# First FFN stage of a fused attention and FFN kernel: 20 block products per 2x3x4 blocks in place of seven per 2x2x2

## The chip, the cores and the metric

One core of a Trainium2 chip runs the whole program. The metric is the time of one execution on the device in microseconds (us).

## The reference

Sigmoid attention over 8 batches of 12 heads, 448 positions and 64 channels, and behind it an FFN without bias on the 3584 tokens (768 to 2048 to 768) with a leaky ReLU, all in float32:

```python
scores = scale * np.matmul(q, k.transpose(0, 1, 3, 2)) - np.log(S)
attn = 1.0 / (1.0 + np.exp(-scores))
attn_out = np.matmul(attn, v)
x = attn_out.transpose(0, 2, 1, 3).reshape(B * S, H * D)
h = x @ w_in
g = np.maximum(0.01 * h, h)
return g @ w_out
```

## The kernel before

The program has three stages in a row. All three keep x, h and the result transposed: channels lie on the 128 partitions, the 448 tokens of a batch in the columns.

*Attention.* 24 rounds of five slots take two pairs of heads each. A round holds scores of two pairs (tiles `sc`, split operands `qks`), the sigmoids on ScalarE (ACT, tiles `s`), and the products with v (`pv`). In the slot after, ACT copies one bank of `pv` to x (`half`) and VectorE (DVE) adds the other bank (`keep`); both banks are then used for later scores. The four PSUM buffers of this stage rotate, so the scores of the next round wait for the two additions.

*Operands in two parts.* Matmuls of the FFN get each float32 operand as a high part (a cast on ACT, method `high`) and a low part (the rest, a subtraction on DVE, `low`), and sum three products: high by high, high by low, low by high. So a product of blocks costs three matmuls for each 128x128 weight block and 448 columns.

*Weights.* `prep` is a generator. It decodes both weight matrices in pieces of 384 elements (load `wr`, five DVE instructions into `wd`), forms sums of blocks, and stores all the forms that the fast schemes need in DRAM (`td` for w_in, `t2d` for w_out). A planner, `prepare` in the attention rounds and `fill` in the first FFN stage, runs as many of its steps in a slot as the time that it counts for DVE there allows. At the end of attention 44 of the 64 pieces are done.

*First FFN stage* (h = x w_in). Four quarters of two batches each; in a quarter four units of 512 columns of w_in. A unit is one 2x2x2 scheme with seven block products in place of eight (`ORDER`). A block has 3 x 128 channels of x, so a product is 2 halves x 3 block columns x 3 parts = 18 matmuls. Class `Quad` keeps the sums: products 0, 4, 3 and 2 share the PSUM tile `px`, product 1 has `py`, 5 and 6 `pz`. `Quad.done` reads partial sums out of PSUM to `c_h` tiles, by an ACT copy where an output begins and a DVE addition where it goes on. A leaky pass on ACT follows, and DVE forms the sums of h that the second FFN stage wants (`made`); all is stored in DRAM. `Operands` makes the sums of x. `Weights` loads a form (`wx`), casts and splits it: `advance` asks for loads eight half products ahead, casts three or four ahead and low parts two or three ahead.

*Second FFN stage.* 52 products of 36 matmuls each in the lanes `acc_A` and `acc_B`, with its own operand and weight queues.

Each engine takes its instructions in the order of the code: `later(n, ...)` puts work in the slot n after, `first=True` ahead of the other work there. All loads and nearly all stores go through the queue of SyncE (SP), in the order of the code as well.

Of the kernel before, what the change touches and what calls it, by code (L numbers as in the profile page):

```python
# [27 lines left out]
GG, OO, WW = 7, 8, (3, 3)  # L28
# [3 lines left out]
PACES = 4, 5, 4.2, 2.8, 2  # L32
TIMES = 1.92, 1.92, 2.33, 2.33, 1.66
PRODUCT, LESS, MOST = 1.8, 0.2, 4
SHORT, LONG, OVER = 0.34, 0.54, 0.1
HOLD, WAIT, REST = 2, 9, 3
FFN = 126
ALONE = 100
LATER = 4
IDLE = 8  # L40


LEFT, MORE, RIGHT = 8, 6, 13

# [59 lines left out]
def attn_ffn_kernel(ctx: ExitStack, tc: tile.TileContext, qk, v, w_in, w_out, out):  # L104
# [18 lines left out]
    NU = w_in.shape[0]  # L123
    HW = NC // 2 * P
    NB = NC // 2
# [5 lines left out]

    td = [tc.dram_tile([P, NOP, 2, HW], F32, name=f"t0_{u}") for u in range(NU // 2)]
    wide = NC // 2 * P
    t2d = tc.dram_tile([P, FORMS, KQ, wide], F32, name="t1")
    xd = [tc.dram_tile([P, NB, S], F32, name=f"xd_{n}") for n in range(4)]
# [7 lines left out]
    mm, dma = pinned(nc.tensor.matmul), pinned(nc.sync.dma_start)  # L143
# [3 lines left out]
    def counted(issue, a_us):  # L147

        def run(out, **kw):
            nonlocal queue  # L150
            queue += 0.14 + math.prod(out.shape[1:]) / a_us
            return issue(out=out, **kw)

        return run
# [30 lines left out]
    stage = left.enter_context(tc.tile_pool(name="stage", bufs=STAGE))  # L185
    ring = left.enter_context(tc.tile_pool(name="ring", bufs=RING))
    prepared = set()

    class Weights:
# [5 lines left out]
        def load(self):  # L195
            self.x = stage.tile([P, 2, HW], F32, tag="stage", name=f"wx{self.u}_{self.n}")
            assert {(0, 2 * self.u), (0, 2 * self.u + 1)} <= prepared
            dma(out=self.x, in_=td[self.u][:, PLACE[self.n]])

        def high(self):  # L200
            self.t = ring.tile([P, 2, 2, HW], F32R, tag="ring", name=f"w0_{self.u}_{self.n}")
            copy(out=self.t[:, :, 0], in_=self.x)

        def low(self):
            sub(self.t[:, :, 1], self.x, self.t[:, :, 0])

    class Wide:
# [6 lines left out]
        def load(self):  # L214
            self.t = self.pool.tile([P, 2, KQ, wide], F32R, tag="t2", name=f"w1_{self.k}")
            dma(out=self.t[:, 1].bitcast(F32), in_=t2d[:, self.form])

        def high(self):
            copy(out=self.t[:, 0], in_=self.t[:, 1].bitcast(F32))
            self.has_high = True  # L220

        def low(self):
            sub(self.t[:, 1], self.t[:, 1].bitcast(F32), self.t[:, 0])
            self.has_low = True

        def of(self, part, e, m):
            return self.t[:, part, e, m * P:m * P + P]

    def parts_mm(acc, w, cols, hi, lo, first, last):

        for n, (part, x) in enumerate(((0, hi), (0, lo), (1, hi))):
            mm(acc, lhsT=w[:, part, cols], rhs=x, start=first and n == 0, stop=last and n == 2,
               skip_group_check=True)

    class Quad:

        def __init__(self, psum, pool, tag, name, bufs, last=copy, tags=("px", "pz")):  # L240


            self.psum, self.pool, self.tag, self.name, self.bufs = psum, pool, tag, name, bufs
            self.last, self.tags = last, tags
            self.x = self.bank(tags[0], "px")

        def bank(self, tag, what):
            return self.psum(tag, f"{what}_{self.name}")[:, :, :S]

        def take(self, what, acc, how=copy):  # L250
            t = self.pool.tile([P, 2, S], F32, tag=self.tag, name=f"{what}_{self.name}", bufs=self.bufs)
            how(out=t, in_=acc)
            return t

        def into(self, n, e):

            if e == 0 and n == 1:
                self.y = self.bank(self.tags[1], "py")
            elif e == 0 and n == 5:
                self.z = self.bank(self.tags[1], "pz")  # L260
            acc = self.y if n == 1 else self.z if n in (5, 6) else self.x
            return acc[:, e], n in (0, 1, 5)

        def done(self, n):

            if n == 0:
                self.c11 = self.take("c11", self.x)
            elif n == 1:
                add(self.c11, self.c11, self.y)
                return 0, 0, self.c11  # L270
            elif n == 4:
                self.c21 = self.take("c21", self.x)
            elif n == 5:
                self.c22 = self.take("c22", self.z)
            elif n == 3:
                add(self.c22, self.c22, self.x)
                return 1, 1, self.c22
            elif n == 6:
                add(self.c21, self.c21, self.z)
                return 1, 0, self.c21  # L280
            elif n == 2:
                return 0, 1, self.take("c12", self.x, self.last)
# [12 lines left out]


    def shift(stack, name, size, side="left"):

# [893 lines left out]
```

## Time and profile before

| | |
|---|---|
| timed runs | 1028.29, 1028.59 (median), 1028.60 us |
| span of the profiled execution, first to last instruction | 1026.2 us |
| TensorE (PE) busy | 1021.9 us |
| DVE busy | 857.5 us |
| ACT busy | 597.4 us |
| moved by DMA | 301.1 MB, mean 293 GB/s |

The span leaves out what lies ahead of the first instruction and behind the last; the median of the timed runs is 2.4 us above it. The time of the profiled execution itself is not recorded apart from its span. "Busy" is the share of time in which an engine had at least one instruction in work. Matmuls overlap in the records, so their pitch is read from the number that start in a stretch. PEld is the load of weights into TensorE, a row of its own in the profile.

### The profile page before, as it was taken

What the parts mean: (1) busy time and instruction counts of PE and PEld (TensorE: products, weight loads), DVE (VectorE), ACT (ScalarE), POOL (GpSimd) and SP (SyncE); (2) the same over time, 40 slices, a digit from 0 to 9 for tenths busy, and PEclk for the clock granted to TensorE, in tenths of its full rate; (3) what the DMA queues carried; (4) which work ended last, traced back from release to release, by engine and by line L of the source; (5) the groups of instructions that cost most, each with busy time, mean ns of one, the idle gap of its engine ahead of it and who ended that gap; (6) DMA issues with size and microseconds to landing.
All of it is one profiled execution on the core that took longest, in us unless ns stands there. A gap on an engine that the chain in (4) does not pass through costs nothing.

```text
span 1026.2 us, 16360 instructions
## 1 busy us (share of the span) xinstructions
PE 1021.9 (100%) x6316; PEld 867.4 (85%) x6316; DVE 857.5 (84%) x1015; ACT 597.4 (58%) x634; POOL 0.3 (0%) x5
## 2 busy tenths in 40 slices
PE   9999999999999999999999999999999999999998
PEld 5555555556999999999999999999999999999998
DVE  5879989889998899898975657699988888899883
ACT  7888888887545555555555555564352535444440
POOL 0000000000000000000000000000000000000000
PEclk9999999999999999999999999999999999999999
DMA  8887778889899998989986878998688797767833
GB/s 311 297 296 273 272 255 273 301 299 347 283 311 324 303 297 312 341 319 409 331 298 217 294 281 322 390 403 293 216 283 286 278 414 290 285 220 253 311 113 135
DMA packets 113853, 301.10 MB, mean 293 GB/s; under 512 B 9712, under 2 KB 51696, under 8 KB 113776
## 3 DMA queue, kind: packets, MB, share of 16 engines
q1 hardware_dynamic: 111760, 295.52, 80.8%
q10 hardware_dynamic: 2016, 4.54, 1.2%
q8 instruction: 50, 0.82, 0.3%
q14 instruction: 27, 0.22, 0.1%
HBM read 203.16 MB, written 96.86 MB: 292 GB/s over the span
## 4 chain that ended last, share of the span: by engine, by line
PE 99%; DMA 0%; SPq 0%; DVE 0%; issue 0%; DVEq 0%
PE px_h L141 22%; PE acc_A L141 18%; PE acc_B L141 18%; PE pv L141 13%; PE pz_h L141 11%; PE sc L141 11%; PE py_h L141 6%; DMA v<-in_v 0%; PE acc_one L141 0%; SPq L141 0%; DVE o L141 0%; DVEq L1188 0%
## 5 line engine op out<-in xcount | busy, mean ns | idle before, releaser
L141 PE MATMUL px_h<-hi,w 128*128 128x448 f32 x768 | 223.0, 361 | 0.0
L141 PEld LDWEIGHTS px_h<-hi,w 128*128 128x128 f32 x768 | 143.9, 187 | 11.4 <-ACT x L141 0.7
L141 PE MATMUL acc_A<-gh,w 128*128 128x448 f32 x528 | 151.4, 361 | 0.0
L141 DVE TENSOR_TENSOR w<-wx,w 128x768 fp32r<-128x768 f32 x112 | 106.9, 954 | 46.3 <-ACT w L141 46.2
L141 PE MATMUL px_h<-lo,w 128*128 128x448 f32 x384 | 139.4, 363 | 0.0
L141 ACT ACTIVATE s<-sc 128x896 f32<-128x896 f32 x144 | 119.4, 934 | 17.3 <-PE sc L141 17.3
L141 PE MATMUL acc_B<-gh,w 128*128 128x448 f32 x416 | 119.4, 361 | 0.0
L141 PE MATMUL pv<-s,v 64*64 64x448 f32 x1152 | 114.0, 540 | 0.2 <-DMA v<-in_v 0.2
L141 PE MATMUL pz_h<-hi,w 128*128 128x448 f32 x384 | 112.7, 361 | 0.0
L141 PEld LDWEIGHTS acc_A<-gh,w 128*128 128x128 f32 x528 | 98.9, 187 | 7.3
L141 PEld LDWEIGHTS sc<-qks 64*128 64x128 f32 x876 | 79.5, 185 | 22.7 <-issue 16.2
L141 ACT CAST w<-wx 128x768 fp32r<-128x768 f32 x112 | 91.9, 833 | 11.0 <-DMA wx<-t 11.0
L141 PE MATMUL sc<-qks 64*128 64x448 f32 (+1 forms) x876 | 94.2, 365 | 0.0
L141 PEld LDWEIGHTS pv<-s,v 64*64 64x64 f32 x1152 | 41.7, 133 | 61.0 <-issue 47.0
L141 DVE TENSOR_TENSOR w<-w 128x1536 fp32r<-128x1536 f32 x52 | 91.1, 1752 | 0.0
L141 ACT ACTIVATE c_h<-c_h 128x896 f32<-128x896 f32 x48 | 45.8, 954 | 74.7 <-DVE c_h L141 74.7
L141 PE MATMUL acc_B<-g,w 128*128 128x448 f32 x328 | 84.8, 362 | 0.0
L141 PEld LDWEIGHTS acc_B<-gh,w 128*128 128x128 f32 x416 | 77.9, 187 | 5.7
L141 ACT CAST w<-w 128x1536 fp32r<-128x1536 f32 x52 | 76.8, 1478 | 0.8 <-DMA w<-t 0.8
L141 PEld LDWEIGHTS pz_h<-hi,w 128*128 128x128 f32 x384 | 71.9, 187 | 5.4
L141 PEld LDWEIGHTS px_h<-lo,w 128*128 128x128 f32 x384 | 72.1, 188 | 3.7
L141 DVE SCALAR_TENSOR_TENSOR wd<-wr,wd 128x384 int32<-128x384 int32 x128 | 71.3, 557 | 3.0
(96 smaller groups left out, 1618.9 us busy)
## 6 DMA issues: line engine op xcount, KB each, us to landing
wx<-t SPq DMA_DIRECT2D x112, 384.0 KB, 5.4
w<-t SPq DMA_DIRECT2D x52, 768.0 KB, 4.4
g<-g SPq DMA_DIRECT2D x34, 896.0 KB, 7.7
g<-c_h SPq DMA_DIRECT2D x60, 448.0 KB, 4.6
g<-s SPq DMA_DIRECT2D x48, 448.0 KB, 5.9
qk<-in_qk SPq DMA_DIRECT2D x46, 456.0 KB, 5.0
g1s<-g SPq DMA_DIRECT2D x18, 896.0 KB, 6.1
wr<-in_w_in SPq DMA_DIRECT2D x32, 384.0 KB, 5.0
```

Of the source, the lines that this page charges most:

```text
L141: return lambda *args, **kw: tc.keep_in_program_order(issue(*args, **kw))
```

## The change

The first FFN stage takes four batches at a time, so it has two halves in place of four quarters. A unit (512 columns of w_in) is now 2 x 3 blocks of w_in by 3 x 4 blocks of x, 24 block products in the plain way, and `PRODUCTS_IN` does them as 20. A block has 2 x 128 channels, so a product is 2 x 2 x 3 = 12 matmuls. Each entry of the table names the lane (a PSUM tile), the form of w_in, the sum of x (`XSUMS`), and the outputs to which the running sum in the lane is added or from which it is taken after this product. Lanes go on after a read, so the value read is a partial sum. There are four PSUM buffers for the five lanes of a unit.

Around it: 16 forms of w_in in place of 7 (`STEPS_IN`), a form being 512 elements a partition where it was 768; 20 sums of x for a half, and x tiles of 896 elements; decoding of two pieces at a time in the attention rounds, instruction by instruction in turn, and in the FFN stage some of its masks on ACT; all memory in named places; another planner (`prepare` in both stages), whose price of a DVE instruction is 0.08 us and 1/960 us an element.

```diff
-ORDER = 0, 1, 4, 5, 3, 6, 2
-NOP = len(ORDER)
-
-PLACE = {0: 1, 1: 2, 4: 3, 5: 4, 3: 5, 6: 6, 2: 0}
-RING, STAGE = 4, 4
-ST = 7
...
+BLOCKS_IN = 4, 5, 0, 1, 2, 3
+FORMS_IN = 16
+STEPS_IN = (
+    ("sum", 3, "sub", ("s", 0, 1), ("d", 2, 0), ("d", 3, 1)), ("sum", 2, "sub", ("s", 3, 1), ("d", 1, 0), ("d", 2, 2)),
+    ("sum", 2, "sub", ("s", 6, 1), ("d", 0, 0), ("d", 3, 2)), ("sum", 1, "sub", ("s", 5, 1), ("d", 3, 1), ("s", 1, 1)),
...
+PRODUCTS_IN = (
+    ("A", 12, 14, "-3"), ("B", 0, 13, ""), ("A", 2, 31, "+1"), ("C", 0, 15, "-5"), ("A", 7, 16, "-0"), ("B", 1, 17, "+0 +4"),
+    ("A", 6, 0, "-4"), ("D", 11, 3, "-7"), ("B", 1, 18, "+7"), ("A", 13, 12, "+5"), ("E", 8, 8, ""), ("E", 10, 4, "-0"),
+    ("C", 15, 27, "-6"), ("B", 14, 21, "+3"), ("E", 8, 20, "-2"), ("C", 10, 29, "-2"), ("B", 9, 25, "+2"), ("E", 4, 23, "-3"),
+    ("C", 5, 28, "-1"), ("B", 3, 2, "+6"))
+N_IN = len(PRODUCTS_IN)
+XSUMS = {
+    12: ("add", 1, 0), 13: ("add", 7, 3), 14: ("sub", 13, 4), 15: ("sub", 14, 5), 16: ("add", 12, 9), 17: ("add", 16, 8),
+    18: ("sub", 11, 17), 19: ("add", 10, 2), 20: ("sub", 19, 8), 21: ("sub", 19, 11), 22: ("sub", 21, 4), 23: ("add", 22, 7),
+    24: ("sub", 22, 5), 25: ("add", 24, 6), 26: ("sub", 25, 21), 27: ("add", 26, 2), 28: ("add", 27, 9), 29: ("add", 27, 5),
+    30: ("add", 16, 14), 31: ("sub", 30, 0)}
+XQUEUE = (
+    "s13 s14 h0 l0 h1 l1 s12 s16 s30 s31 h2 l2 s15 h3 l3 h4 l4 s17 h5 l5 h6 l6 h7 l7 s18 h8 l8 h9 l9 h10 l10 h11 l11 "
...
+            both = 2 - k % 2 if now < FFN else 1
...
+            chains = [decode(raws[at + n][0], dec[:, (k + n) * PIECE:(k + n + 1) * PIECE], at + n in bare) for n in range(both)]
+            while chains:
+                for x in list(chains):
+                    step = next(x, None)
+                    if step is None:
+                        chains.remove(x)
+                    else:
...
-        while at_high < len(w1) and w1[at_high][0] <= t + 3 + (t >= 7):
+        while at_high < highs:
             w1[at_high][1].high()
             at_high += 1
-        while at_low < len(w1) and w1[at_low][0] <= t + 2 + (t >= 7):
+        while at_low < lows:
             w1[at_low][1].low()
             at_low += 1
-        while at_load < len(w1) and w1[at_load][0] <= t + 8 and at_load < at_low + STAGE:
+        while at_load < min(loads, at_low + RAWS):
             w1[at_load][1].load()
             at_load += 1
...
-            t = (self.p + 1) * NU * NOP - len(self.todo)
-            u, n, e = self.todo.pop(0)
-            advance(t)
-            p = self.p
-            if n == ORDER[0] and e == 0:
-                self.quad = Quad(psum, st, "st", f"h{p}_{u}", ST, leaky)
-                self.c = Results()
-            quad, c = self.quad, self.c
-            w = w1[t // 2][1].t[:, e]
-            acc, first = quad.into(n, e)
-            hi, lo = self.ops.hi[n], self.ops.lo[n]
-            for kk in range(NB):
-                parts_mm(acc, w, slice(kk * P, kk * P + P), hi[:, kk], lo[:, kk], first and kk == 0, kk == NB - 1)
-            if e == 0:
+            n = self.n
+            self.n += 1
+            t = N_IN * (UI * self.p + self.u) + n
+            x_ops(t)
+            advance(before(t + 7), before(t + 3), before(t + 2))
+            lane = PRODUCTS_IN[n][0]
+            first = lane not in self.accs
+            if first:
+                bank = lanes.pop(0)
+                self.accs[lane] = bank, psum(bank, f"acc_{t}")
+            bank, acc = self.accs[lane]
+            w, b = of_product[t], blocks[self.p]
+            hi, lo = b.forms[n].hi, b.forms[n].lo
+            for e in range(2):
+                for kk in range(NB):
+                    cols = slice(kk * P, kk * P + P)
+                    for m, (a, x) in enumerate(((w.hi, hi), (w.hi, lo), (w.lo, hi))):
+                        mm(acc[:, e, :S], lhsT=a[:, e, cols], rhs=x[:, kk], start=first and kk == 0 and m == 0,
+                           stop=kk == NB - 1 and m == 2, skip_group_check=True)
+            if self.u == UI - 1:
+                b.used(n)
+            ends = all(x[0] != lane for x in PRODUCTS_IN[n + 1:])
+            later(1, lambda: self.read(n, acc, bank, ends), first=True)
+
+        def read(self, n, acc, bank, ends):
+            for x in PRODUCTS_IN[n][3].split():
+                sign, o = x[0], divmod(int(x[1:]), 4)
+                if o not in self.outs:
+                    i, t = o
+                    name = self.names[t // 2][i, t % 2]
+                    users = 1 + sum(name in y[2:] for y in self.sums[t // 2])
+                    r = self.outs[o] = Result(f"h{self.p}_{self.u}_{i}{t}", users)
+                    if sign == "+":
+                        copy(out=r.t, in_=acc[:, :, :S])
+                    else:
+                        act(out=r.t, in_=acc[:, :, :S], func=AF.Copy, scale=-1.0)
+                else:
+                    r = self.outs[o]
+                    (add if sign == "+" else sub)(r.t, r.t, acc[:, :, :S])
+                if self.last[o] == n:
+                    self.done(o, r)
+            if ends:
+                lanes.append(bank)
...
-    wi = moe_w_in.reshape(2, NC // 2, P, 2, NU, P).transpose(4, 2, 0, 3, 1, 5).reshape(NU, P, 4, HW)
-    wi = np.ascontiguousarray(wi[:, :, [1, 3, 0, 2]]).reshape(NU, P, 4 * HW).view(np.int64)
+    wi = moe_w_in.reshape(3, 2, P, 2, NU // 2, 2, P).transpose(4, 5, 2, 3, 0, 1, 6).reshape(NU, P, len(BLOCKS_IN), 2 * P)
+    wi = np.ascontiguousarray(wi[:, :, list(BLOCKS_IN)]).reshape(NU, P, 4 * HW).view(np.int64)
```

Where instructions stand. DVE, attention stage, the decoding of the third unit of w_in (`wr` is a raw piece, `wd` the decoded one; in the rows of the changed kernel `wde`; `qks` the low part of q and k). Before:

```order
L141 TENSOR_SCALAR wd_2_840<-wr_2_1_654 128x384
L141 TENSOR_SCALAR wd_2_840<-wd_2_840 128x384 x2
L141 SCALAR_TENSOR_TENSOR wd_2_840<-wr_2_1_654,wd_2_840 128x384 x2
L141 TENSOR_SCALAR wd_2_840<-wr_2_2_676 128x384
L141 TENSOR_SCALAR wd_2_840<-wd_2_840 128x384 x2
L141 SCALAR_TENSOR_TENSOR wd_2_840<-wr_2_2_676,wd_2_840 128x384
L141 TENSOR_TENSOR qks_913<-qk_754,qks_913 128x848
L141 SCALAR_TENSOR_TENSOR wd_2_840<-wr_2_2_676,wd_2_840 128x384
```

And of the change:

```order
L188 TENSOR_SCALAR wde_321<-wr_2_0_465 128x384
L188 TENSOR_SCALAR wde_321<-wr_2_1_467 128x384
L188 TENSOR_SCALAR wde_321<-wde_321 128x384 x4
L188 SCALAR_TENSOR_TENSOR wde_321<-wr_2_0_465,wde_321 128x384
L188 SCALAR_TENSOR_TENSOR wde_321<-wr_2_1_467,wde_321 128x384
L188 SCALAR_TENSOR_TENSOR wde_321<-wr_2_0_465,wde_321 128x384
L188 SCALAR_TENSOR_TENSOR wde_321<-wr_2_1_467,wde_321 128x384
L188 TENSOR_TENSOR qks_845<-qk_677,qks_845 128x848
```

Each instruction on a piece had the one before it on the same piece as its neighbour; now the other piece stands between them.

TensorE, the first products of the first FFN stage (`hi`, `lo` and `f` are x operands, `w` weights). Before, the end of the first product and the start of the second:

```order
L141 MATMUL px_h_0_3280<-hi_0_1066,w_0_0_3215 128x448 x2
L141 MATMUL px_h_0_3280<-lo_0_1135,w_0_0_3215 128x448
L141 MATMUL px_h_0_3280<-hi_0_1066,w_0_0_3215 128x448
L141 MATMUL py_h_0_3317<-hi_0_1322,w_0_1_3242 128x448
L141 MATMUL py_h_0_3317<-lo_0_1390,w_0_1_3242 128x448
L141 MATMUL py_h_0_3317<-hi_0_1322,w_0_1_3242 128x448 x2
```

And of the change, the first ten products, one row each:

```order
L188 MATMUL acc_3409<-f_0_1929,w_0_12_3338 128x448 x12
L188 MATMUL acc_3437<-f_0_2060,w_0_0_3357 128x448 x12
L188 MATMUL acc_3409<-f_0_2454,w_0_2_3400 128x448 x12
L188 MATMUL acc_3482<-f_0_2585,w_0_0_3357 128x448 x12
L188 MATMUL acc_3409<-f_0_2714,w_0_7_3435 128x448 x12
L188 MATMUL acc_3437<-f_0_2847,w_0_1_3455 128x448 x12
L188 MATMUL acc_3409<-f_0_2971,w_0_6_3477 128x448 x12
L188 MATMUL acc_3563<-f_0_3104,w_0_11_3499 128x448 x12
L188 MATMUL acc_3437<-f_0_3396,w_0_1_3455 128x448 x12
L188 MATMUL acc_3409<-f_0_3398,w_0_13_3542 128x448 x12
```

A product has 12 matmuls where it had 18, and the tile `acc_3409` (lane A) comes back after one other product three times.

ACT, the same place. Before:

```order
L141 COPY c_h_0_3310<-px_h_0_3280 128x896
L141 CAST hi_0_3312<-x_825 128x1344
L141 CAST w_0_5_3330<-wx_5_3240 128x2x384
L141 ACTIVATE c_h_0_3310<-c_h_0_3310 128x896
L141 CAST hi_0_3359<-x_446 128x1344
L141 CAST w_0_3_3361<-wx_3_3257 128x2x384
L141 COPY c_h_0_3372<-px_h_0_3280 128x896
```

And of the change (`h` is an output, `acc` its lane):

```order
L188 ACTIVATE h_0_03_3427<-acc_3409 128x896
L188 CAST f_0_3430<-x_606 128x896
L188 CAST f_0_3433<-x_470 128x896
L188 CAST w_0_7_3435<-wx_7_3368 128x512
L188 CAST w_0_1_3455<-wx_1_3403 128x512
L188 COPY h_0_01_3472<-acc_3409 128x896
L188 CAST w_0_6_3477<-wx_6_3405 128x512
L188 ACTIVATE h_0_11_3495<-acc_3482 128x896
```

Between two reads of one PSUM tile by ACT stood four passes, and now stand four shorter ones within two products of 12 matmuls.

## Rows read from the trace of the kernel before

**Rows 1.** The page: span; then busy us (share of the span) and instructions.

```profile
span 1026.2 us, 16360 instructions
...
PE 1021.9 (100%) x6316; PEld 867.4 (85%) x6316; DVE 857.5 (84%) x1015; ACT 597.4 (58%) x634; POOL 0.3 (0%) x5
```

**Rows 2.** The chain that ended last, in time: start us, us, what.

```profile
1.65 4.96 DMA v<-in_v
...
19.86 4.67 PE pv L141 x48
...
29.85 4.67 PE pv L141 x48
...
266.87 7.20 PE px_h L141 x36
```

**Rows 3.** Windows of the three stages: busy us of each engine, granted clock, DMA share, GB/s.

```profile
0.00:244.50 244.50, 243.56 (x2424) 138.65 (x2428) 204.45 (x391) 205.38 (x268) 0.30 (x5) 1.00 0.84 290
244.50:648.00 403.50, 403.50 (x2023) 377.74 (x2016) 332.85 (x437) 221.07 (x251) 0.00 (x0) 1.00 0.89 313
648.00:1026.00 378.00, 374.87 (x1875) 351.02 (x1873) 320.21 (x188) 170.91 (x116) 0.00 (x0) 1.00 0.75 276
```

**Rows 4.** The waits: who for whom, us in total, times, longest us.

```profile
ACT c_h L141 <- DVE c_h L141: 74.7, 45, 2.6
...
DVE qks L141 <- ACT qks L141: 21.5, 22, 4.1
...
ACT w L141 <- DMA wx<-t: 11.0, 8, 2.7
...
PEld pv L141 <- ACT s L141: 8.8, 27, 0.5
...
PEld px_h L141 <- ACT x L141: 0.7, 1, 0.7
```

**Rows 5.** Windows of an attention round and of seven products; columns as in rows 3.

```profile
124.80:134.70 9.90, 9.90 (x108) 5.56 (x104) 9.69 (x19) 8.34 (x12) 0.00 (x0) 1.00 0.72 245
...
446.10:471.30 25.20, 25.20 (x127) 23.62 (x127) 23.56 (x35) 14.18 (x16) 0.00 (x0) 1.00 0.96 359
```

**Rows 6.** Groups of DVE by shape: count, busy us, mean ns, idle before.

```profile
L141 DVE TENSOR_TENSOR w<-wx,w 128x768 fp32r<-128x768 f32 x112 | 106.9, 954 | 46.3 <-ACT w L141 46.2
...
L141 DVE TENSOR_TENSOR lo<-x,hi 128x1344 fp32r<-128x1344 f32 x24 | 37.2, 1552 | 1.0 <-ACT hi L141 1.0
...
L141 DVE TENSOR_TENSOR x<-x,pv 128x448 f32<-128x448 f32 x48 | 27.6, 616 | 4.7 <-PE pv L141 4.3
...
L141 DVE TENSOR_TENSOR wd<-wd 128x192 f32<-128x192 f32 x56 | 19.2, 353 | 2.5 <-DMA t<-wd 2.2
...
L141 DVE TENSOR_TENSOR c_h<-c_h,px_h 128x896 f32<-128x896 f32 x16 | 17.3, 1083 | 3.6 <-PE px_h L141 3.4
...
L141 DVE TENSOR_TENSOR wd<-wd 128x576 f32<-128x576 f32 x8 | 6.1, 756 | 0.2
```

**Rows 7.** Timeline of DVE in one round: start us, us, instruction, count.

```profile
61.30 0.75 DVE L141 TENSOR_SCALAR wd<-wd 128x384 f32<-128x384 f32 x2
...
62.76 1.04 DVE L141 TENSOR_TENSOR qks<-qk,qks 128x848 fp32r<-128x848 f32 x1
63.72 0.55 DVE L141 SCALAR_TENSOR_TENSOR wd<-wr,wd 128x384 int32<-128x384 int32 x1
64.19 0.35 DVE L141 TENSOR_SCALAR wd<-wr 128x384 int32<-128x384 int32 x1
64.46 1.03 DVE L141 TENSOR_TENSOR qks<-qk,qks 128x848 fp32r<-128x848 f32 x1
```

**Rows 8.** Groups of ACT by shape; columns as in rows 6.

```profile
L141 ACT CAST w<-wx 128x768 fp32r<-128x768 f32 x112 | 91.9, 833 | 11.0 <-DMA wx<-t 11.0
...
L141 ACT ACTIVATE c_h<-c_h 128x896 f32<-128x896 f32 x48 | 45.8, 954 | 74.7 <-DVE c_h L141 74.7
```

**Rows 9.** DMA issues: count, KB each, median us from issue to landing.

```profile
wx<-t SPq DMA_DIRECT2D x112, 384.0 KB, 5.4
```

More of the change, by code (lines that the diff above doesn't have):

```diff
@@ L220, in high @@
             self.has_high = True
         def low(self):
-            sub(self.t[:, 1], self.t[:, 1].bitcast(F32), self.t[:, 0])
+            sub(self.lo, self.raw, self.hi)
             self.has_low = True
         def of(self, part, e, m):
[L227 to L282, printed above, removed]
@@ L452, in prep @@
                 prepared.add((w, u))
-                if w == 0:
-                    yield from rest()
     preps = prep()
-    def prepare(pace, time, ends):
-        nonlocal credit, queue, ahead
-        credit += pace
-        while credit >= 1 and now >= hold and queue < time - LESS:
-            if ends and queue + ahead > time + OVER:
-                later(0, after, first=True)
-                queue += ahead
-            else:
-                ahead = next(preps, None) or SHORT
-            credit -= 1
-        queue = max(0.0, queue - time)
@@ L471, in after, with prepare @@
[L471 to L485 removed]
+    paused = len(FIRST_UNITS)
+    def prepare(time, ends=False, less=LESS):
+        nonlocal queue, ahead
+        while now >= hold and ahead < math.inf and queue + ends * ahead <= time - less:
+            ahead = next(preps, math.inf)
+        queue = max(0.0, queue - time)
@@ L785, in attn_ffn_kernel @@
     pairs[3].load_qk()
-    ops = [Operands(q) for q in range(NQ)]
     psum = banks("ps_a", dict(s=(4, 2)))
-    def go(todo, work):
-        for x, what in todo:
-            for y in what.split():
-                later(0, lambda x=x, y=y: x.do(y))
-        slot(work)
     def whole(x):
@@ new lines, in attn_ffn_kernel @@
+    slots.extend((fm, f"m{n}") for n in range(4))
+    xv = pool(left, "xv")
+    spares.extend((*shared.values(), (xv, "x")))
+    psum = banks("ps_f", {x: (1, 2) for x in "abcd"})
+    for x in "abcd":
+        psum(x, f"first_{x}")
+    lanes = ["d", "c", "a", "b"]
+    queue = 0.0
+    for p in range(2):
+        for u in range(UI):
+            if (p, u) == (1, UI - 1):
+                break
+            first = First(p, u)
+            for n in range(N_IN):
+                if (p, u) == (0, UI - 1):
+                    for i in RELOAD_AT.get(n, ()):
+                        later(0, lambda i=i: blocks[1].load(i))
+                if p == 0:
+                    for x in AHEAD_AT.get(n + N_IN * (u - UI + 2), ()):
+                        later(0, lambda x=x: blocks[1].ahead(x))
+                if paused == 2 and not blocks[0].queue or paused == 1 and not blocks[1].queue:
+                    paused, ahead = paused - 1, 0.0
+                slot(first.step)
+                prepare(PRODUCT, less=EASE[p])
@@ L1013, in g_load @@
             ahead += 1
-    weights = [Wide(k, t2a) for k in range(WW[0])]
+    WW = 3
+    weights = []
     todo = [(operands[k], "load") for k in range(READY)]
@@ L1083, in read, with w_load @@
                     store(p, o)
-    g_load(-1)
-    for x in weights[WW[0]:AHEAD]:
-        x.load()
+    asked = WW
+    def w_load(n):
+        nonlocal asked
+        for x in weights[asked:n]:
+            x.load()
+        asked = max(asked, min(n, total))
+    w_load(WW + 1)
     for k in range(total):
```

822 lines of the change are left out of this document (501 added, 321 removed), and 7 rows, old and new, of tables (ROUND_OPS, STEPS_IN).

## The prediction

> **What bounds the kernel now.** I read the page's busy times first, then the chain that ended last, then the windows, then the waits. The page gives TensorE (PE) 1021.9 us of a span of 1026.2 us [rows 1]; since matmuls overlap in the records, a busy PE alone proves little, so the pitch is read from the chain. In the first FFN stage 36 matmuls of 448 columns take 7.20 us, which is 0.200 us each [rows 2]. [...] A round of the attention stage takes 9.99 us (19.86 to 29.85) [rows 2].
>
> The other engines follow. VectorE (DVE) is busy 204.45, 332.85 and 320.21 us in the three stages, so 84, 82 and 85%; ScalarE (ACT) 205.38, 221.07 and 170.91 [rows 3]. They have slack on the average, less in places: one round has DVE at 9.69 of 9.90 us, and an early window of the FFN stage 23.56 of 25.20 [rows 5]. In both windows PE is busy throughout. DVE and ACT wait for one another and for DMA; PE's weight loads wait for ACT 8.8 us in 27 places of the attention stage, 0.5 at most and inside the rounds of 9.99, and 0.7 us where the FFN stage begins [rows 4]. That is the state that the change must keep: DVE may run at 93 to 98% of a stretch without costing anything.
>
> **The change: what it removes.** The new scheme has 2 halves x 4 units x 20 products, each of 2 x 2 x 3 = 12 matmuls of the same shape (the order shows `x12` a row). That is 1920 matmuls. 96 x 0.200 us = **19.2 us** less on PE, all of it on the path that sets the end; the stage should take 384.0 us. Attention and the second FFN stage keep their matmul counts (1652 and 1872 instructions).
>
> **What it adds on DVE.** I priced the instructions that the two orders show per stage. A price here is start to start: behind an independent neighbour the next instruction begins 0.08 us before the last one ends (848 elements: 1.04 us long, the next starts 0.96 us later; 384: 0.55 and 0.47; tensor_scalar: 0.35 and 0.27), while a dependent one begins after it (two in 0.75 us, so 0.39 apart) [rows 7]. So from the mean durations [rows 6]: 1344 elements 1.47, 896 1.00, 768 0.87, 384 0.47, 192 0.27. Two shapes are not in the trace. 512 elements lie between 448 (0.616 long) and 576 (0.756): 0.686, so 0.61 start to start. 256 lie between 192 (0.353) and 384 (0.55): 0.42, so 0.34. Both ends are so near that they move nothing.
>
> [...]
>
> Attention stage, DVE, change in counts: +20 of 896 (sums of x), +19 of 512, +48 of 256 and +6 of 768 (sums of weight blocks), +6 of 192, -8 of 1344, -31 of 384 (four casts fewer of q and k are left out). That is 20.0 + 11.6 + 16.3 + 5.2 + 1.6 - 11.8 - 14.6 = +28.3 us. Against it stands the decoding of the weights: two pieces now alternate, so that neighbours no longer depend on each other; in this stage the order has 18 dependent neighbours in place of 158, and 140 x 0.12 = 16.8 us fall away. Net +11.5 us: 216 us if the interleaving counts in full, 233 if not at all. Over 23 rounds that is +0.5 to +1.2 us on a mean of 8.35 (204.45 of 244.5 us, a round being 9.99), so 8.9 to 9.6 of 9.99. I take the low end, since the rows show both pitches; even the high end lies under the 9.69 that a round has carried [rows 5]. So I cost it at nothing. The cover is the queue of DVE at the end of a round: the two `keep` additions must be done before the next scores reuse their banks. What lies above 9.99 in a round goes to PE one for one.
>
> First FFN stage, DVE: +100 of 896, +125 of 512, -110 of 768, -36 of 1344, -15 tensor_scalar, -6 of 192, -1 of 384: 100.0 + 76.3 - 95.7 - 52.9 - 4.1 - 1.6 - 0.5 = +21.5 us, less 12 dependent pairs, so +20. DVE comes to 353 of 384 us, 92% where it was 82%. Summed by unit of 20 products (48.0 us of PE) the rows of the order give 46, 38, 39, 46, 49, 41, 46 and 39 us. So seven units are like the early windows of before, and the fifth (first of the second half, with its sums of x) has 49 in 48: **1.0 us** that I charge to PE. Below nothing it can't go; above, the deadlines bound it: a low part of a weight is issued two products ahead, 4.8 us, where it was three half products, 5.4; less its own length that leaves 4.1 us where 4.4 were. PE can lose what DVE is late beyond 4.1 us, at most a few us in that unit.
>
> **ACT and DMA.** In the FFN stage ACT has 109 casts of 768 (0.833) and 23 of 1344 fewer, and 125 of 512 (0.56, in proportion to 768 with nothing fixed, to 0.833), 30 of 896, 15 of 384 and 18 reads of PSUM or leaky passes of 896 (0.95) more [rows 8]: at the high end 104 + 45 + 7 less 91 and some 30, so +35 on 221.07, 256 of 384 us. In eight of the later attention rounds it has one cast of 896 more, below 0.95 on a mean of 8.4 (205.38 of 244.5): under 9.99. Loads of weights carry 256 KB in place of 384 and land in a median 5.4 us [rows 9]; they are asked for up to 7 products (16.8 us) ahead but by four buffers at most, and cast 3 ahead. ACT waited for them 11.0 us in eight places before [rows 4] without PE noticing. SP's queue gets 55 more DMAs, mainly smaller weight loads and the x tiles. By the sizes in the two orders the FFN stage moves 120 MB in 384 us, before 124 in 403; in attention 80 MB go where 72 went, 326 GB/s where the trace has 290, while the FFN stage ran at 313 without a wait [rows 3]. I leave it at nothing, with one load late by half its 5.4 us as the upper bound, some 3 us.
>
> **Sum.** The profiled span is 1026.2 us; the timed runs have 1028.59 as median, 2.4 us outside the span, which I keep. 1026.2 - 19.2 + 1.0 = 1008.0, and with 2.4: **1010.4 us**, 1.8% faster.
>
> **Rivals.** *1. DVE binds in stretches.* For it: waits of DVE for ACT's casts of q and k, 21.5 us in 22 places [rows 4], come on top of fuller rounds, and `keep` is then late in each. At the high end 233 us of work and 21.5 of waits stand in the stage's 244.5 us, of which the start (5 us of loading [rows 2]) gives DVE nothing: 15 late. Against it: when DVE is behind, the cast is done before it asks, and the wait is gone. Some 60% of it gives +9: 1019.5.
> *2. Instructions of DVE that don't overlap.* If each began only when the one before had ended, the stage's counts times the full durations count: 255 us for attention (224 before), in 244.5 less 5 of loading, 15 late; and the fifth FFN unit, with 55 instructions, gains 55 x 0.08 and holds 53 us in 48, 5 late. 1028.6 - 19.2 + 20 = 1029.4. Against it stand the starts in [rows 7]. [...]
> *3. Slower: the partial reads of PSUM.* In lane A the products 0, 2 and 4 of a unit are read by ACT while only one other product runs: 2.4 us, where a bank had 3.6. If ACT stands at a leaky pass waiting for DVE (up to 2.6 us, 74.7 us in 45 places [rows 4]), then needs 0.95 for it and 0.95 for the read, PE waits 2.6 + 0.95 + 0.95 - 2.4 = 2.1 us. 24 such places at half that price are 25 us: 1034. It decides from 0.8 us a place. Against it: the read stands first in its slot, and two of three leaky passes are issued elsewhere.
> *4. The second FFN stage starts late.* Its memory opens after product 6 of the last unit, 33.6 us ahead, and its first weight (768 KB, so 10.8 us by twice a 384 KB load [rows 9]) must be loaded, cast and split, some 15 us: room enough unless the load is held in SP's queue for 18 us; at +7, 1017.
>
> **Chances.** Forecast 0.64 (its own range 1008.6 to 1013), rival 1 0.20, rival 4 0.05, rival 2 0.04, rival 3 0.07. The low end has the 0.7 us wait at the stage's start gone and half of the unit's excess absorbed. The range that holds 8 in 10 runs from **1008.6 to 1019.5**. Within 0.2% (2 us, about what a measurement of this kernel can tell from no change) is rival 2 and the full price of rival 1, 0.05; slower is rival 3 and a little of rival 2, 0.08; faster 0.87.
>
> **What would show it.** Right: the chain still 99% PE, 2.40 us per 12 matmuls, the FFN stage 384 to 386 us, rounds of 9.99 us. DVE near 350 us there. Wrong: PEld or PE waiting for DVE (`w`, `x`, `h`) or ACT with more than 2 us in total; rounds longer than 10.0 us mean rival 1, gaps behind products 1, 3 and 5 of a unit rival 3, a gap before the first `acc` of the second stage rival 4.

## The result: 1.15% slower, and the profile after

The changed kernel takes 1040.17 us as median of 4 runs (1038.87 to 1042.22), the kernel before 1028.44 beside it: a ratio of 1.0115, 95% interval 1.01 to 1.013. The forecast was 1010.4 with a range of 1008.6 to 1019.5: the time lies outside it, and on the wrong side of the kernel before. The page of the profiled execution (its own time 1038.87 us), which answers to [rows 1]:

```profile
span 1037.1 us, 16483 instructions
...
PE 1014.0 (98%) x6220; PEld 848.6 (82%) x6220; DVE 888.6 (86%) x1128; ACT 606.4 (58%) x699; POOL 0.3 (0%) x5
```

PE has 96 matmuls fewer and is idle for the first time: 98% where it was 100. The windows of the three stages, with the columns of [rows 3]:

```profile
0.00:250.30 250.30, 246.64 (x2428) 138.81 (x2428) 219.12 (x450) 210.24 (x277) 0.30 (x5) 1.00 0.92 320
250.30:655.60 405.30, 391.71 (x1924) 359.14 (x1920) 347.60 (x489) 225.28 (x307) 0.00 (x0) 1.00 0.85 297
655.60:1037.00 381.40, 375.63 (x1873) 350.64 (x1872) 321.91 (x189) 170.89 (x116) 0.00 (x0) 1.00 0.74 275
```

The work came out as priced: VectorE (DVE) has 219.1 and 347.6 us (forecast 216 and 353), and the pitch of matmuls is still 0.200 us, 7.20 for 36. But the first FFN stage lasts 406.5 us from its first matmul to the next stage's first, not 385. By the starts of its matmuls, 384.0 are pitch and 22.5 are what neighbours stand further apart than 0.200 us: 0.9, 1.6, 0.0, 4.6, 4.0, 2.6, 2.1 and 5.4 in the eight units, and 1.3 ahead of the next stage's first. (Products are numbered through the stage from 0, 20 to a unit; product 96, in the fifth unit, alone loses 3.6.) Attention gives the stage over 5.4 us later than before, and the second FFN stage is 2.3 us longer. Against the forecast's span of 1008.0 that is 5.4 + 21.5 + 2.3 = 29.2 of 29.1 us.

The waits in the first FFN stage, which answer to [rows 4]: who for whom, us in total, times, longest.

```profile
DVE s L188 <- DMA g<-s: 10.3, 4, 3.5
DVE early L188 <- DMA early<-xd: 6.3, 3, 4.5
DVE wdw L188 <- DMA wr<-in_w_out: 3.5, 1, 3.5
...
ACT h L188 <- DMA g<-h: 15.7, 6, 3.8
ACT w L188 <- DMA wx<-t: 14.4, 9, 3.4
ACT w L188 <- DMA w<-t: 8.7, 2, 5.6
ACT wdw L188 <- DMA wr<-in_w_out: 7.3, 8, 1.3
...
PEld acc L188 <- DVE w L188: 11.0, 12, 2.3
PEld acc L188 <- ACT h L188: 7.5, 8, 1.5
```

The rows that name a DMA add to 66 us. `g<-h` and `g<-s` are stores of result tiles: the engine wants to write a tile whose last content is still on its way out. The last two rows are what PE's weight loads wait for in turn: low parts of weights from DVE, and banks that ACT has not read. Before, no row of DVE in this stage names a DMA, and ScalarE (ACT) waited 15.3 us, all for weights: the 11.0 of [rows 4] and

```profile
ACT c_h L141 <- DMA wx<-t: 4.3, 3, 2.2
```

The timeline shows what a wait for a store does: start us, us, instruction, and in brackets its idle time before and what ended it.

```profile
303.33 0.41 SPq L196 DMA_DIRECT2D g<-h  x1
...
308.47 0.91 ACT L188 COPY h<-acc 128x896 f32<-128x896 f32 x1 [3.84 <-DMA g<-h]
...
309.21 1.09 DVE L188 TENSOR_TENSOR s<-s,h 128x896 f32<-128x896 f32 x1 [3.54 <-DMA g<-s]
...
309.43 4.70 PEld L188 LDWEIGHTS acc<-f,w 128*128 128x128 f32 x24 [0.79 <-ACT h L188]
```

A store issued at 303.33 has landed at 308.4; ACT, which works in order, stands in front of the read of PSUM for 3.84 us, then PE's weight load waits 0.79 us for the bank. In attention it is decoding that stands (2.23 us, at a store of its tile) ahead of the additions `x<-x,pv` (`keep`) that free the banks of the next scores, and PE waits 0.94 us for these:

```profile
38.61 0.63 DVE L188 TENSOR_SCALAR wde<-wr 128x384 int32<-128x384 int32 x2 [2.23 <-DMA t<-wde]
39.16 1.14 DVE L188 TENSOR_TENSOR x<-x,pv 128x448 f32<-128x448 f32 x2
...
39.82 2.48 PE L188 MATMUL sc<-qks 64*128 64x448 f32 x22 [0.94 <-DVE x L188]
```

Three rounds are 1.1 to 1.3 us too long for this reason; behind the start the others keep to 9.99 within 0.3. And in the last unit both engines stand at the wide weights (`w<-t`, 768 KB) of the second FFN stage. The load whose cast waits 5.58 us was issued at 624.83, 13.5 us ahead of the cast:

```profile
624.83 0.48 SPq L196 DMA_DIRECT2D w<-t  x1
...
638.38 1.48 ACT L188 CAST w<-w 128x1536 fp32r<-128x1536 f32 x1 [5.58 <-DMA w<-t]
...
639.90 1.76 DVE L188 TENSOR_TENSOR w<-w 128x1536 fp32r<-128x1536 f32 x1 [4.40 <-ACT w L188]
...
646.25 0.90 PEld L188 LDWEIGHTS acc<-f,w 128*128 128x128 f32 x5 [2.28 <-DVE w L188]
```

### The profile page after: what moved, and what is told of

The parts are those of the page before. It is cut to its first block, busy times and chain, and to the rows that moved or that the text cites. A ratio compares the mean times of both kernels' runs of the same rounds, so it can differ in the third digit from the quotient of the medians.

```text
span 1037.1 us, 16483 instructions
## 1 busy us (share of the span) xinstructions
PE 1014.0 (98%) x6220; PEld 848.6 (82%) x6220; DVE 888.6 (86%) x1128; ACT 606.4 (58%) x699; POOL 0.3 (0%) x5
## 5 line engine op out<-in xcount | busy, mean ns | idle before, releaser
L188 PE MATMUL acc<-f,w 128*128 128x448 f32 x1920 | 391.8, 364 | 13.6 <-DVE w L188 7.2
L188 PEld LDWEIGHTS acc<-f,w 128*128 128x128 f32 x1920 | 359.1, 188 | 46.6 <-DVE w L188 11.0
L188 DVE TENSOR_TENSOR h<-h,acc 128x896 f32<-128x896 f32 x88 | 95.3, 1083 | 15.8 <-PE acc L188 7.3
L188 DVE TENSOR_TENSOR w<-wx,w 128x512 fp32r<-128x512 f32 x128 | 86.9, 685 | 5.3 <-ACT w L188 5.3
L188 ACT CAST w<-wx 128x512 fp32r<-128x512 f32 x128 | 76.1, 616 | 26.1 <-DMA wx<-t 14.4
L188 ACT ACTIVATE h<-h 128x896 f32<-128x896 f32 x64 | 60.8, 950 | 34.4 <-DVE h L188 31.6
L188 ACT ACTIVATE h<-acc 128x896 f32<-128x896 f32 x48 | 44.1, 918 | 42.0 <-PE acc L188 38.0
L188 PE MATMUL acc_A<-g1s,w 128*128 128x448 f32 x192 | 65.9, 362 | 0.0
L188 PEld LDWEIGHTS acc_B<-g,w 128*128 128x128 f32 x328 | 61.5, 187 | 4.2
L188 DVE TENSOR_TENSOR qks<-qk,qks 128x848 fp32r<-128x848 f32 (+3 forms) x51 | 50.2, 987 | 13.9 <-ACT qks L188 13.6
## 6 DMA issues: line engine op xcount, KB each, us to landing
wr<-in_w_in SPq DMA_DIRECT2D x32, 384.0 KB, 6.0
```

Source lines behind the costliest of these rows:

```text
L188: return lambda *args, **kw: tc.keep_in_program_order(issue(*args, **kw))
```

## The experiments

Theory 1: DVE and ACT, which work in order, stand at DMAs whose data or tiles are late, and what PE needs is queued behind. Theory 2: DVE has too much to do. Theory 3 (rival 3): banks come back late because of the short windows for ACT's reads. e1 to e18 are the runs in the order of the record. A result is the ratio to the kernel before, run on the same chip, with its 95% interval in brackets; the changed kernel has 1.0115. The passages set off in each group are what was expected of its runs before they ran, in the order of their numbers. Traces are of one execution each, and executions of one of these kernels differ by 2 to 8 us, so a trace shows where time goes and the ratio what a move is worth.

**One move each.** Four kernels, each with one move:

```diff
-            later(2, lambda: save(name, r))           # e1
+            later(1, lambda: save(name, r, dma_act))
-    26: (('sum', 15, 3, 1, 3),),                      # e2; 19 to 24 one key later
+    29: (('sum', 15, 3, 1, 3),),
-T2_AT = (0, 0, "load"), (2, 0, "high"), (3, 0, "low"), ...   # e3; all three weights
+T2_AT = (0, 0, "load"), (4, 0, "high"), (5, 0, "low"), ...
-        while now >= hold and ahead ...               # e4
+        while now >= hold + (ends and now < STRICT) and ahead ...
```

> One part of the changed kernel is moved: each plain result tile of the first FFN stage is stored by a DMA that ScalarE issues right behind its leaky pass, where SP's queue issued it a slot later, behind weight loads that wait for VectorE. Work, matmuls and bytes stay the same. Theory 1 (VectorE and ScalarE, which work in order, stand at DMAs whose data or tiles come late, and PE's margins are shorter than such a wait): the waits of ScalarE for the stores of result tiles (15.7 us in the stage) and of VectorE (10.3 us) fall to under half, the waits of PE at 309, 315, 562 and 573 us go, and the time falls by 2 to 4 us. Theory 2 (VectorE has too much to do): no change beyond 1 us. Theory 3 (PSUM banks that are handed back late because ScalarE reads them in 2.4 us): no change, since the order of reads stays.

> In the changed kernel the additions of the second half's x tiles, which VectorE does in the third and fourth unit of the first FFN stage, stand one product later (the last of them three), their loads stay where they are but for one that follows its tile by one product. Theory 1 (in-order engines that stand at late DMAs): VectorE's waits for these loads (6.3 us in 3 places, 4.5 the longest) go, the fourth unit's loss (4.6 us, products 60 to 69) falls by 2 to 4 us and the time with it. Theory 2 (VectorE's load): the same additions in the same units, no change beyond 1 us. Theory 3 (PSUM banks): no change.

> In the changed kernel the casts and differences of the second FFN stage's first three weights stand 4 and 5 products behind their loads, where they stood 2 and 3 behind; the loads stay. Theory 1 (in-order engines that stand at late DMAs): ScalarE's waits for the wide loads (8.7 us in 2 places) and those of VectorE behind them (7.3 us) go, the last unit, which loses 5.4 us and 1.3 more at the next stage's first matmul, loses 1 to 2 us, and the time falls by 4 to 5 us. Theory 2 (VectorE's load): the last unit has the same work, no change beyond 1 us. Theory 3 (PSUM banks): the losses in products 11, 15 and 16 stay.

> In the changed kernel's attention stage, weight decoding that overwrites a tile whose store may still be under way is issued one slot later where it would stand at the end of a round, ahead of the two additions that free the banks of the next scores. Theory 1 (in-order engines that stand at late DMAs): VectorE's waits for the stores of the decoded tile (6.2 us in 4 places) no longer stand ahead of these additions, the rounds of 11.1 to 11.3 us become 9.99, the first FFN stage starts at 246 to 247 us where it started at 250.4, and the time falls by 3 to 4 us. Theory 2 (VectorE has too much to do in a round): the long rounds stay or move to other places, no change beyond 1 us.

Measured: e1 1.0066 (1.005 to 1.0082), e2 1.0115 (1.0101 to 1.0129), e3 1.0062 (1.0049 to 1.0075), e4 1.0065 (1.0053 to 1.0078). So three moves give some 5 us each and one nothing. In e1 the gaps at products 24, 26 and 124 are gone (that at 128 stays) although every bank is read by the same engine in the same order: what made these reads late was the tile, which speaks against theory 3. ACT's wait for stores halves, DVE's hardly changes (its tiles hold sums, which SP still stores):

```profile
DVE s L188 <- DMA g<-s: 8.9, 4, 3.4
...
ACT h L188 <- DMA g<-h: 7.8, 3, 4.4
```

In e4 the three long rounds last 9.99 and the FFN stage starts at 247.3 us, the wait of DVE for the decoded tile (6.2 us in 4 places without the move) being

```profile
DVE wde L188 <- DMA t<-wde: 1.8, 4, 0.6
```

In e3 ACT's wait for wide weights falls from 8.7 to 1.5 us, though a new one of 3.0 (a cast for the second FFN stage, which stands at the load of its operand, with a cast of weights behind it) costs 2.8 us in product 13 of the last unit. e2 is a miss of theory 1: the waits for x did go and the fourth unit's gaps fell from 4.6 to 0.8 us, but the fifth unit's grew from 4.0 to 7.4. That unit is where theory 2 holds: in the changed kernel's trace DVE has no idle time in the ten us up to the gap in product 96, which loses 3.6 us (windows, columns as in [rows 3]). From 450 to 490 us DVE makes sums of x, of h and low parts and decodes nothing, so less decoding (e6, below) can't lighten it, and product 96 loses 2.2 to 2.3 us in e6 as in e1, e3 and e4:

```profile
480.00:485.00 5.00, 5.00 (x27) 4.69 (x26) 5.00 (x7) 4.27 (x5) 0.00 (x0) 1.00 0.69 249
485.00:490.00 5.00, 3.62 (x19) 3.04 (x17) 5.00 (x6) 1.51 (x3) 0.00 (x0) 1.00 0.21 82
```

**The three moves together, and less work for DVE.**

> The changed kernel with three moves at once: result tiles stored by ScalarE behind their leaky pass (first experiment), the first three wide weights cast and split two products later (third), decoding that overwrites a tile under store kept out of a round's end (fourth). Work and bytes unchanged. Theory 1 (in-order engines at late DMAs): the places differ, so the gains add: 3 us in attention, 6 us from the result tiles and 3 to 4 us in the last unit, and the half clock of 3.4 us that followed PE's longest wait is rarer: 1025 to 1029 us, about the time of the kernel before. Theory 2 (VectorE's load): the waits move to other places, over 1031 us.

> The changed kernel without the last three of the five steps that decode a piece of a weight, in the first FFN stage alone (the shift and the two that join the halves of a double), so the second FFN stage computes with other numbers. Every load, store, cast and the order of all that is left stays. VectorE has 29 us less to do in that stage (40 x 0.556 + 20 x 0.360), 318 us in place of 348. Theory 1 (in-order engines at late DMAs): the stage still loses 14 to 20 of its 22.5 us, since the waits for DMAs stay; 1033 to 1039 us. Theory 2 (VectorE's load): the loss falls below 8 us; under 1027 us.

> The three moves and the lighter decoding together (the decoding leaves out what the run before left out). If waits of the first kind and the load of VectorE are all that stands between the kernel and the forecast, the first FFN stage comes to 384 to 390 us and the time to 1013 to 1020 us. Theory 1 alone would have it near the run with the three moves (within 3 us), theory 2 alone near the run with less decoding.

> The three moves, and the planner of weight decoding stops at 2.2 us of VectorE's work in a product of the second half of the first FFN stage, where it stopped at 2.3; what is left over is decoded later in the same half. The work is the same. Theory 1: within 2 us of the run with the three moves. Theory 2: units six to eight, which lose 6 to 10 us in all, lose 2 to 5 us less.

```diff
+        if now >= FFN:                                # e6, e7: in decode()
+            yield cost(PIECE)
+            yield cost(PIECE)
+            return
-EASE = 0.35, LESS                                     # e8
+EASE = 0.35, 0.2
```

Measured: e5 0.9979 (0.997 to 0.9987, 1026.70 us), e6 1.0052 (1.0032 to 1.0073, 1034.37 us), e7 1.0021 (1.0011 to 1.0032), e8 0.9974 (0.9963 to 0.9984). The three moves add up: 14.0 us by the ratios (12.3 by the spans of the traces), where the single ones sum to 15.6 by theirs. The FFN stage of e6 by windows (first row), of e5 (second):

```profile
250.30:654.20 403.90, 391.93 (x1924) 361.18 (x1920) 322.67 (x431) 224.27 (x307) 0.00 (x0) 0.99 0.85 299
```

```profile
247.00:644.80 397.80, 387.56 (x1924) 358.71 (x1920) 348.41 (x491) 229.06 (x307) 0.00 (x0) 1.00 0.86 303
```

In these traces e6 takes 25 us of work from DVE and the stage still loses 20 us; e5 takes nothing from it and the stage loses 13.9. So theory 2 is not the main cause. Nor is DVE's load nothing: by the ratios e6 is 6.5 us below the changed kernel, about as much as one of the three moves gives (its trace is of its slowest execution, 1037.21 us, with two falls of the clock). Through which places it gains that is not shown. e8 differs from e5 by less than the intervals, where theory 2 expected 2 to 5 us. e7, lighter and with the moves, is slower than e5 by 0.4%, which neither theory had; its first FFN stage takes 401.5 us where the expectation had 384 to 390, so late DMAs in these three places and the load of decoding are not all that keeps the kernel from the forecast. PE loses 5.1 us in its seventh unit, and ACT stands longer at raw weights (`wr`) than in e5, whose row follows:

```profile
ACT wdw L188 <- DMA wr<-in_w_out: 16.9, 6, 4.7
```

```profile
ACT wdw L188 <- DMA wr<-in_w_out: 4.8, 5, 1.6
```

That a DVE which is earlier gives the in-order queues less cover, so that the missing work made the wait longer, is argued from these rows, not tried apart.

**Tiles.** One result tile fewer in the kernel before (`ST = 7` to `6`); in the changed kernel ten for nine, with the memory of one of the five buffers for cast weights (`STS` 9 to 10, `CASTS` 5 to 4), alone and with the three moves.

> The kernel before, with six result tiles of the first FFN stage in place of seven; nothing else. In its own trace VectorE waits for no DMA in that stage and ScalarE 15.3 us in 11 places for weights, none for a result tile under store. Theory 1 (in-order engines at late DMAs): with a tile less such waits appear in this kernel as well, and PE then waits too although VectorE has the same 333 us to do: 2 to 15 us slower. Theory 2 (VectorE's load): no change beyond 1 us.

> The changed kernel with ten result tiles in place of nine; the memory is that of one of the five buffers for weights that are cast and split, which are four then. No instruction moves on any engine. Theory 1 (in-order engines at late DMAs): the waits for stores of result tiles (ScalarE's 15.7 and VectorE's 10.3 us) nearly vanish, the losses in products 24, 26, 124 and 128 with them, 3 to 6 us less than the changed kernel on the same chip, if four buffers for weights are enough; if they aren't, waits of ScalarE for PE at casts take their place and the loss goes up. Theory 2 (VectorE's load): no change beyond 1 us.

> The three moves and ten result tiles (four buffers for cast weights). Theory 1: what waits for stores of result tiles are left with the three moves (VectorE 9.7 us for sums) go; the losses that followed from them in the sixth and seventh unit fall by 1 to 3 us, so 1 to 3 us less than the three moves, 1023 to 1026 us.

Measured: e9 1.0098 (1.0083 to 1.0113), e14 1.0229 (1.0215 to 1.0243), e15 1.01 (1.0085 to 1.0115). e9 brings waits of the changed kernel's kind into the kernel before, with its work untouched. Its waits, then the timeline of the worst place:

```profile
DVE s L141 <- DMA g<-s: 21.6, 5, 9.9
```

```profile
471.55 2.22 DVE L141 TENSOR_TENSOR s<-s,c_h 128x896 f32<-128x896 f32 x2 [9.86 <-DMA g<-s]
...
472.72 0.91 ACT L141 COPY c_h<-pz_h 128x896 f32<-128x896 f32 x1 [8.01 <-DVE s L141]
...
473.68 0.29 PEld L141 LDWEIGHTS pz_h<-hi,w 128*128 128x128 f32 x1 [6.61 <-ACT c_h L141]
```

DVE waits for a tile, ACT for DVE, PE for ACT. e14 takes the waits for stores of result tiles in the stage from 27 us to 12, but ACT then waits for PE to release a buffer of cast weights, and PE for low parts:

```profile
ACT w L188 <- PE acc L188: 33.5, 17, 4.4
PEld acc L188 <- DVE w L188: 17.8, 23, 2.5
```

against 11.0 us of the latter in the changed kernel. So neither pool has a buffer to spare, and in this exchange the cast buffer was worth more than the tile. e15 repeats it from the better start: its expectation missed by 13 us.

**Other moves on top of the three.** Sums stored by ACT too and the last x addition two products later (e10), raw weights counted as landed three slots behind their load (e11), the limit of e8 (e12); then the same without the stores by ACT (e13, e17).

```diff
-                later(1, lambda: save(x, new))        # e10, e11, e12
+                later(1, lambda: save(x, new, dma_act))
-    26: (('sum', 15, 3, 1, 3),),                      # e10 to e13, e17
+    28: (('sum', 15, 3, 1, 3),),
-            raws.append((raw, now + (LAG if now < FFN else 2)))     # e11, e13
+            raws.append((raw, now + (LAG if now < FFN else 2 + (now > FFN + 100))))
```

> The three moves, and two more: the sums of result tiles are stored by ScalarE too, and the last of the additions of the second half's x tiles stands two products later. Theory 1: VectorE's waits for stores of sums (9.7 us in 4 places) and for the last x tile (3.5 of 5.5 us) fall; products 69 and 108 lose up to 2 us less in all, 1023 to 1027 us; less of a gain if ScalarE now stands at sums that VectorE has not made yet. Theory 2: no change beyond 1 us against the three moves.

> The four moves, and raw weights of the last two and a half units are counted as landed three slots behind their load, where it was two. Theory 1: VectorE's wait of 2.8 us for a raw weight at 511 us goes, and with it the 2.9 us that PE loses in products 108 and 109; 1020 to 1025 us. Theory 2: within 1 us of the run before it.

> The four moves, and the planner's limit of 2.2 us a product in the second half. Theory 1: within 2 us of the four moves; by the run with three moves and this limit, 1 us less: 1021 to 1026 us.

> The three moves, with the last addition of the second half's x tiles two products later and raw weights of the last two and a half units counted as landed three slots behind their load; sums are stored through SP's queue as in the changed kernel. Theory 1 (in-order engines at late DMAs): the wait of 3.5 us for the last x tile and that of 2.8 us for a raw weight go, and with them up to 1.1 us in product 69 and 2.9 in products 108 and 109; 2 to 4 us less than the three moves have on the same chip.

> The three moves, the last addition of the second half's x tiles two products later, and the planner's limit of 2.2 us a product in the second half; no raw weight is delayed and no sum stored by ScalarE. Theory 1: product 69 loses 1.1 us less, units six to eight 1 to 2 us less than with the three moves alone: 1 to 3 us below the run beside it on the same chip.

Measured: e10 1.0098 (1.0084 to 1.0111), e11 1.011 (1.0096 to 1.0124), e12 1.0082 (1.0068 to 1.0096): all three are misses, 11 to 13 us above the three moves by the ratios. The granted clock was 0.99 to 0.995 on the mean in these runs, 0.997 to 1.0 in e5's; how much of the loss that makes was not tried apart. e12 and e17 (below) differ in one line alone, the queue that stores the sums: 1.0082 against 0.9967, so ACT's queue is the worse place for them by 11.8 us. In e10, where DVE stands 8.19 us at the store of a sum that ACT issues, ACT waits 5.55 us for DVE, and PE 4.33 us at 311.9; in the second FFN stage PE waits 6.57 us for ACT:

```profile
310.13 1.09 DVE L188 TENSOR_TENSOR s<-s,h 128x896 f32<-128x896 f32 x1 [8.19 <-DMA g<-s]
...
311.63 0.55 ACT L188 ACTIVATE wdw<-wr 128x384 f32<-128x384 f32 x1 [5.55 <-DVE s L188]
...
311.88 6.10 PEld L188 LDWEIGHTS acc<-f,w 128*128 128x128 f32 x17 [4.33 <-DVE w L188]
...
671.49 0.29 PEld L188 LDWEIGHTS acc_A<-gh,w 128*128 128x128 f32 x1 [6.57 <-ACT o L188]
```

e13 has 1.0033 (1.002 to 1.0045): the gaps at products 69, 108 and 109 went as expected, but the decoding that was put off lands in the last unit, which loses 7.3 us where e5 lost none. e17 has **0.9967** (0.9954 to 0.998, 1025.88 us), the lowest ratio, though its interval overlaps e8's: product 69 and units seven and eight lose nothing. But the stage as a whole loses 14.1 us in e17's trace, 13.9 in e5's: the fourth unit still has a gap of 3.8 us at product 62 (2.8 in e5) and the fifth unit loses 6.1, with a fall of the clock in each. So this trace does not show where e17's gain lies. At product 62 ACT stands at a load of weights; in e5:

```profile
396.55 0.62 ACT L188 CAST w<-wx 128x512 fp32r<-128x512 f32 x1 [5.28 <-DMA wx<-t]
...
399.39 17.11 PEld L188 LDWEIGHTS acc<-f,w 128*128 128x128 f32 x86 [2.85 <-ACT h L188]
```

ACT's waits for these loads are 18.9 us in e5 and 14.4 in the changed kernel, and no run moves them.

**Repeats.**

> The changed kernel as it is, for the comparison on one chip with the runs beside it and for its granted clock: 1037 to 1042 us, with more time in the executions in which the clock falls to half behind a wait of PE (some 1.7 us for each fall of 3.4 us).

> The kernel with the three moves once more, as it ran in the fifth experiment. If that result holds, 0.1 to 0.3% below the kernel before; if the clock falls more often on this chip, level with it (some 1.7 us for each fall of 3.4 us).

e16 1.0108 (1.0093 to 1.0124), beside e13 to e15; e18 0.9994 (0.9986 to 1.0003), beside e17. The three moves alone are thus level with the kernel before or 0.2% below it, and e17 is below e18, by 1.4 us.

## Why the prediction was wrong, point by point

- **What is removed** held: 2016 less 1920 are 96 matmuls at 0.200 us (before, 2016 at this pitch made 403.2 of the stage's 403.5 us [rows 3]), and the granted clock is 1.00 in all three stages but for a short fall (last section). Attention has 2428 matmuls in both kernels, not the 1652 of the text; only that they are equal was used.
- **What it adds on DVE** held in sum (219.1 and 347.6 us; the prediction's rows by unit add to 344, not to its 353). So did the length of 512 elements that it put between two shapes, 0.686 us: in the changed kernel's trace the 128 instructions `w<-wx,w` of 512 have a mean of 0.685. The fifth unit's 1.0 us was under-sized: the unit loses 3.1 to 3.2 us in e1, e3 to e7 and e16, which have no fall of the clock there, and 4.0 in the changed kernel's trace, which has one. That it is the unit bound by DVE was foreseen.
- **The step that failed is "ACT and DMA", "I leave it at nothing, with one load late by half its 5.4 us as the upper bound, some 3 us".** It asked whether weights land in time, whether ACT has room and what the DMA moves on the mean, and took the stage before to run "without a wait", which is so of PE but not of ACT (15.3 us). It left out the waits at the head of an in-order engine: a unit's eight results are now summed over its 20 products in nine tiles, where seven tiles served four results at a time, so that the next tile can be one whose store is under way (27 us of waits, where e1 halves ACT's part and takes 5.0 us off the time); decoding overwrites a tile under store at a round's end (e4, 5.1 us); and casts stand two products, 4.8 us, behind the wide loads, of which one took 13.5 us (e3, 5.5 us). These three are 14 of the 29 us by e5's ratio, 12 by its trace. For the other half no run isolates a cause, and no run's median comes nearer to the forecast than 15 us. By the traces, so argued: fifth unit 2 to 4, x tiles and loads of weights in the fourth unit some 4, raw weights 3 (x tiles and raw weights were moved in e13, only for the decoding to come due later), falls of the clock, and the start of attention 1.8 and of the second FFN stage 2.3, which were not tried.
- **The margin** was in the text: a low part has 4.1 us where 4.4 were. A wait of 2 to 5 us at the head of an in-order engine (2.23 to 5.58 in the rows above) takes half of that or all of it; the bound should have been made from such waits, not from throughput.
- **Rival 1** (DVE binds in stretches; 1019.5) is right for one unit, and its "`keep` is late" came true in three rounds, from a store and not from load. **Rival 2** fell: neighbours still overlap in the changed kernel (two of 896 elements, 1.08 us long each, take 2.09 us at 482.8). **Rival 3** was the right side for another reason: PE did wait for ACT's reads behind products 3 and 5, but e1 removes the gaps at 24, 26 and 124 with the reads left as they were, and behind the gap at product 62 stands a load of weights; in the places looked at the 2.4 us windows cost nothing until something stops ACT. (The order before shows five passes of ACT between two reads of `px`, not four.) **Rival 4**: the stage's first matmul waited 1.3 us (DVE `h`), no load was late for it; the price of the wide weights was paid ahead of that, in the last unit of the first stage, by products that stood behind their casts.

## What to carry to other kernels

When a change holds tiles longer or packs more engines' work into one in-order queue, list for each instruction at the head of DVE and ACT which DMA it can stand at (a load, or the store that still reads its tile) and what PE needs behind it; DVE's busy share of the stage, 82% before and 86% after, did not show the 22.5 us that the stage lost. Take stores close behind the instruction that makes the data, on the engine that made it (e1, 5.0 us), and put filling work and casts of far-off data well behind the landing of their DMA (e3, 5.5 us, and e4, 5.1); but with the stores of DVE's sums on ACT's queue the kernel was 11.8 us slower (e12 against e17). A tile fewer cost 1% in e9, so a scheme's memory is part of its price.

## What was not expected of the hardware

The granted clock fell to 0.50 in or behind some gaps of PE. In the changed kernel PE was idle for most of 489 to 491 us and then ran at a granted clock of 0.50 for the length of the third window:

```profile
484.00:489.00 5.00, 4.62 (x24) 3.98 (x22) 5.00 (x6) 2.07 (x3) 0.00 (x0) 1.00 0.41 163
489.00:491.00 2.00, 0.43 (x2) 0.41 (x3) 2.00 (x3) 1.05 (x2) 0.00 (x0) 0.99 0.00 0
491.00:494.00 3.00, 3.00 (x10) 2.65 (x9) 2.12 (x3) 3.00 (x6) 0.00 (x0) 0.50 0.78 235
494.00:497.00 3.00, 3.00 (x16) 2.79 (x15) 3.00 (x5) 0.79 (x3) 0.00 (x0) 0.94 0.85 254
```

10 matmuls are in work in these 3 us and 16 in the next. Product 96 loses 3.6 us here and 2.3 in e1, where the clock stays at 1.00 behind a gap at the same place that is no shorter (first row of the changed kernel, second of e1):

```profile
490.57 1.69 PEld L188 LDWEIGHTS acc<-f,w 128*128 128x128 f32 x6 [2.33 <-DVE w L188]
```

```profile
488.20 1.91 PEld L188 LDWEIGHTS acc<-f,w 128*128 128x128 f32 x10 [2.37 <-DVE w L188]
```

So the fall cost 1.3 us here, and it did not follow every such gap. In e9 the clock falls within the gap of 6.6 us and is 0.50 from 470 to 480 us:

```profile
470.00:475.00 5.00, 1.32 (x3) 0.81 (x4) 3.41 (x5) 2.28 (x3) 0.00 (x0) 0.50 0.32 128
475.00:480.00 5.00, 5.00 (x14) 4.44 (x14) 4.96 (x9) 2.99 (x4) 0.00 (x0) 0.50 1.03 328
```

In the second row PE is busy throughout and has 14 matmuls in 5 us, where the pitch of 0.200 us makes 25. So in both kernels PE paid for a wait a second time. The clock is only a part of the spread between executions: e1's run from 1031.78 us (mean granted clock 1.0) to 1037.43 (0.997), and 0.003 of the clock is at most some 3 us of these 5.7; in e5 two executions at 1.0 have 1023.51 and 1027.46 us. The kernel before, beside e1, runs from 1027.91 to 1028.81. What else spreads the others was not tried; that the waits themselves differ from one execution to the next is a guess.
